# Chunk 1's DMA transposes made to wait for chunk 2's softmax-weight spread: a study of one ordering change

## The chip, the cores and the metric

The kernel runs on one core of one Trainium2 chip. The metric is the device time of one execution in microseconds (us). Each median below is over all runs of one kernel in one comparison. A ratio is the mean time of one kernel's fast runs over that of the other's fast runs of the same rounds on the same chip, so it is not quite the ratio of the two medians quoted beside it. Runs of three or more rounds are given with a 95% interval of that ratio.

## The reference, cut to what matters

Two layers with a residual each, over 2048 positions of width 1024 in bf16:

```python
def _A_ref(x, wqkv, wo):            # 32 heads of 32; each position attends to 8 earlier ones, 2 apart
    ...
    logits = jnp.where(mask[None, None, :, :], logits, -1000000000.0)
    attn = _softmax(logits, axis=-1)
    o = jnp.einsum('bhsw,bhswd->bhsd', attn, vg)
    return (...)(o, 0, 2, 1, 3).reshape(B, S, D) @ wo

def _B_ref(x, w_in, w_sp, b_sp, w_out):
    z = _gelu(jnp.einsum('bsd,df->bsf', x, w_in))
    z1 = z[..., :Fh].copy()
    z2 = _layernorm(z[..., Fh:], axis=-1)
    g = jnp.einsum('ts,bsf->btf', w_sp, z2) + b_sp[None, :, None]
    return jnp.einsum('bsf,fd->bsd', z1 * g, w_out)

h  = x + _A_ref(_layernorm(x, axis=-1), A_wqkv, A_wo)
h2 = h + _B_ref(_layernorm(h, axis=-1), B_w_in, B_w_sp, B_b_sp, B_w_out)
```

The layer norm of `h` is called LN2 here.

## The kernel before: the parts that the change and the argument touch

The positions are worked in four chunks of 512 (four blocks of 128 each). The author plans the order of the instructions of the tensor engine (PE), the vector engine (DVE) and the scalar engine (ACT) with a small list scheduler, `Order`: each `add` names an engine, an estimated duration, a function that emits the instructions, and the operations it depends on. `dma_op` is an operation on a pretend engine "DMA". The functions are called in the order of their planned starts. The queues of SP and GpSimd (POOL), which issue most transfers, the build orders itself. `behind(i, j, why)` makes instruction i wait on the chip until transfer j has landed.

The three places that matter are the spread of the softmax weights, the transposes of LN2's output, and the stores of z1:

```python
# attention(c): softmax weights of a chunk, copied from 32 rows per quarter to 128 rows, in two halves
for q in (0, 2, 1, 3):
    i_ = (A.dma_start if hw == 0 and q < 2 else dma_w)(
        st["AB"][:, hw, q]..., st["attn"][32 * q:32 * q + 32, ws, :]....to_broadcast([H, 4, 512]))
    if hw == 0:
        st["sent", q] = i_
    else:
        behind(i_, st["sent", 1], "second half behind the first")
        behind(i_, st["sent", 3], "second half behind the first")
...
# head(c): LN2's normalised output is transposed by DMA, one block at a time, from SP
for il in range(TPC):
    def tr(il=il):
        ...
        G["hntr"] = nc.sync.dma_start_transpose(hnTs[c][:, il], st["hnc"][:, il, :]....)
        if c == NCH - 3:
            behind(G["hntr"], G["ld", c + 2, 1], "transposing and loading by turns")
    trs.append(dma_op(4.0, tr, [nd[il]]))
...
# b_z1(c): ACT evicts an accumulator through GELU into one of four buffers, SP stores it
def ev(fp=fp):
    z1s = l1.tile([P, 2, CH], BF16, name="z1s", tag="xn", bufs=4)
    A.activation(z1s[:], G["accy", c, fp][:], ACTF.Gelu_apprx_tanh)
    last_store[:] = [dma(z1_d[2 * fp:2 * fp + 2, ...], z1s[:])]
```

The transposed LN2 output of chunk 1 (`hnT`) is read by PE in `b_z2(1)`, block by block. PE's accumulators (`acc`) are three buffers, each freed by an eviction on ACT or DVE.

## Time and profile before

| What | Value | Where it is read |
|---|---|---|
| time | 723.0 us median (722.67 to 724.84, 6 runs) | the runs beside the changed kernel's |
| PE busy | 716.1 us of a 721.3 us span, clock 1.0 | the page |
| unbroken row of matmuls in the chain | 7.42 to 718.32 us | the chain, in order of time |
| waits of PE | 1.3 and 0.7 us, both in the start-up | who waited for whom |
| four transposes of chunk 1 | issued from 240.57 to 247.56 us | timeline |
| PE's first use of block 0, of block 1 | 254.15, 260.21 us | timeline |

First, two lines of the page of the kernel before: PE's busy time, and the engines' shares of the chain of work that ended last.

```profile
PE 716.1 (99%) x3449; PEld 364.0 (50%) x3449; DVE 412.2 (57%) x442; ACT 236.1 (33%) x301; POOL 63.8 (9%) x78
...
PE 99%; DVE 0%; DMA 0%; ACT 0%; issue 0%
```

The same chain in order of time (start, duration, what; L666 is the output projection, L736 is z2, L786 is z1, L896 is the spatial mix), around the place of the change and later:

```profile
234.35 19.96 PE acc L786 x92
254.32 24.21 PE acc L736 x128
...
286.30 13.81 PE acc L666 x64
...
428.19 48.35 PE acc L896 x224
```

The pieces join without a hole: 234.35 + 19.96 is 254.31, and so on. 224 matmuls in 48.35 us are 215.9 ns each. The Trainium skill ("TensorE: Matmul & The Clock Gate", "Step-by-step: what each phase is for") has about 216 ns for the gap of back-to-back matmuls of 512 columns, and this trace agrees. PE neither waits nor runs slowly, so as long as its work stays the same, no other engine's saving can shorten this row.

Now the place itself: the timeline of the kernel before from 200 to 262 us (start, duration, engine, line, operation, output and input, count; in brackets, how long the engine was idle before and what ended that; SPq and ACTq are the instruction queues of SP and ACT, here issuing transfers).

```profile
240.57 6.99 SPq L708 DMA_TRANSPOSE hnT<-hb  x4
240.78 1.26 ACTq L558 DMA_DIRECT2D AB<-attn  x2
...
241.16 1.12 POOL L558 DMA_DIRECT2D AB<-attn  x2 [8.81 <-PE acc L786]
...
246.90 2.17 POOL L558 DMA_DIRECT2D AB<-attn  x4 [4.62 <-DVE l3var L628]
...
247.66 5.96 SPq L793 DMA_DIRECT2D z_d<-z1s  x5
...
249.91 2.28 DVE L604 TENSOR_TENSOR oT<-vT,AB 128x4096 bf16<-128x4096 bf16 x1
...
252.21 1.02 ACT L792 ACTIVATE z1s<-acc 128x1024 bf16<-128x1024 f32 x1 [3.67 <-DMA z_d<-z1s]
...
254.15 3.62 PE L736 MATMUL acc<-win_1453,hnT 128*128 128x512 bf16 x16
...
260.21 2.10 PE L736 MATMUL acc<-win_1453,hnT 128*128 128x512 bf16 x9
```

The four transposes stand in a row on SP from 240.57 us; the trace's list of SP's waits has them released by the load of chunk 3's keys (`kT`). The first half of the spread goes out beside them (ACT's queue from 240.78, POOL's from 241.16), and its second half follows at 246.90, once the first has landed. The bracket on that line names DVE, but by the code these transfers depend on the first half and not on that DVE instruction (in e5 below the same bracket names the transfer). Five stores of z1 stand behind the transposes, and ACT waits 3.67 us for the landing of one of them before the eviction at 252.21. DVE starts on the spread weights at 249.91 without a wait. The four transposes took 4.0 to 5.5 us from issue to landing; those of the other chunks took 2.9 us in the median.

### The profile page before, as it was taken

Reading aid. Unit: us, or ns where it says so; the run is one execution under the profiler, and the core shown is the slowest. Engines: PE = TensorE matmul, PEld = TensorE weight load, DVE = VectorE, ACT = ScalarE, POOL = GpSimd, SP = SyncE. Lnnn points to the kernel's source line nnn. Section 1 sums busy time; section 2 is a strip of 40 time slices with the busy share of each in tenths; the row PEclk is TensorE's granted clock in tenths of the full one; section 3 lists DMA queues with packets and bytes.
Section 4 is the critical chain, followed back from the end, with each engine's and each line's share of the span. In section 5 each row is a group of like instructions: output and inputs, shape, how many; then the busy total and the mean of one; then the engine's idle time right before and its main releaser. Section 6 shows DMA issues by size and latency. Waiting matters only on the chain.

```text
span 721.3 us, 8471 instructions
## 1 busy us (share of the span) xinstructions
PE 716.1 (99%) x3449; PEld 364.0 (50%) x3449; DVE 412.2 (57%) x442; ACT 236.1 (33%) x301; POOL 63.8 (9%) x78
## 2 busy tenths in 40 slices
PE   8999999999999999999999999999999999999998
PEld 4666665666644454445445444444444444444444
DVE  5898799979998999887961203222222222222222
ACT  4389452532447595766725420000000000000000
POOL 0011400012002302201113000000000000000000
PEclk9999999999999999999999999999999999999999
DMA  9995765567662942642336989463015311120002
GB/s 330 268 286 141 219 153 163 162 199 247 239 238 86 238 174 90 234 117 59 143 119 195 279 227 306 144 149 114 30 44 135 126 32 45 33 88 11 1 16 72
DMA packets 119990, 107.35 MB, mean 149 GB/s; under 512 B 72896, under 2 KB 98272, under 8 KB 119952
## 3 DMA queue, kind: packets, MB, share of 16 engines
q1 hardware_dynamic: 110624, 73.95, 34.9%
q0 software_dynamic: 7888, 31.43, 13.1%
q10 hardware_dynamic: 1440, 1.44, 0.8%
q8 instruction: 27, 0.44, 0.3%
q14 instruction: 11, 0.09, 0.0%
HBM read 55.09 MB, written 30.74 MB: 119 GB/s over the span
## 4 chain that ended last, share of the span: by engine, by line
PE 99%; DVE 0%; DMA 0%; ACT 0%; issue 0%
PE acc L896 27%; PE acc L393 21%; PE acc L736 13%; PE acc L786 13%; PE acc L918 13%; PE acc L666 8%; PE acc L303 2%; PE L L501 1%; DMA xp<-in_A_x_dram 0%; PE tpa L265 0%; DVE xn L253 0%; DVE bnst L241 0%; DVE bnst L242 0%; DVE ot L920 0%; ACT xnT L267 0%
## 5 line engine op out<-in xcount | busy, mean ns | idle before, releaser
L736 PEld LDWEIGHTS <-hnT 128*128 128x128 bf16 x512 | 50.0, 98 | 47.3 <-issue 0.4
L918 PEld LDWEIGHTS <-zg 128*128 128x128 bf16 x462 | 45.2, 98 | 51.8
L449 DVE TENSOR_TENSOR prod<-qT,kT 128x4096 bf16<-128x4096 bf16 (+1 forms) x32 | 68.2, 2152 | 2.7 <-ACT kT L399 1.5
L604 DVE TENSOR_TENSOR prod<-vT,AB 128x4096 bf16<-128x4096 bf16 (+1 forms) x32 | 64.3, 2022 | 0.8
L606 DVE TENSOR_TENSOR oT<-oT,prod 128x4096 bf16<-128x4096 bf16 (+1 forms) x32 | 64.5, 2018 | 0.1
L920 DVE TENSOR_TENSOR ot<-acc,hr 128x1024 bf16<-128x1024 f32 (+2 forms) x18 | 19.9, 1106 | 73.1 <-PE acc L918 73.1
L918 PE MATMUL acc<-wout_a,zg 128*128 128x512 bf16 (+1 forms) x264 | 58.2, 373 | 0.0
L736 PE MATMUL acc<-win_1453,hnT 128*128 128x512 bf16 x256 | 58.2, 379 | 0.0
L393 PE MATMUL acc<-xnT,wk 128*128 128x512 bf16 x256 | 56.3, 379 | 0.0
L786 PE MATMUL acc<-hnT,win_1657 128*128 128x512 bf16 x256 | 56.2, 379 | 0.0
L666 PE MATMUL acc<-wo_sb,oT 128*128 128x512 bf16 x256 | 56.1, 379 | 0.0
L393 PE MATMUL acc<-xnT,wv 128*128 128x512 bf16 x256 | 55.9, 379 | 0.0
L404 ACT CAST stg<-acc 128x1024 bf16<-128x1024 f32 x36 | 36.4, 1011 | 58.4 <-PE acc L393 51.5
L393 PEld LDWEIGHTS <-wk 128*128 128x128 bf16 x256 | 36.9, 145 | 18.6 <-issue 0.4
L393 PEld LDWEIGHTS <-wv 128*128 128x128 bf16 x256 | 37.0, 145 | 18.2
L918 PE MATMUL acc<-wout_b,zg 128*128 128x512 bf16 (+1 forms) x198 | 44.4, 373 | 0.0
L736 PE MATMUL acc<-win_1550,hnT 128*128 128x512 bf16 (+1 forms) x256 | 44.2, 326 | 0.0
L786 PE MATMUL acc<-hnT,win_1663 128*128 128x512 bf16 x192 | 42.4, 379 | 0.0
L393 PE MATMUL acc<-xnT,wq 128*128 128x512 bf16 x192 | 42.2, 379 | 0.0
L792 ACT ACTIVATE z1s<-acc 128x1024 bf16<-128x1024 f32 x28 | 28.5, 1020 | 38.6 <-PE acc L786 30.2
L666 PEld LDWEIGHTS <-oT 128*128 128x128 bf16 x256 | 25.0, 98 | 30.2
L786 PEld LDWEIGHTS <-win_1657 128*128 128x128 bf16 x256 | 25.0, 98 | 30.0 <-issue 0.4
(267 smaller groups left out, 968.3 us busy)
## 6 DMA issues: line engine op xcount, KB each, us to landing
z_d<-z1s SPq DMA_DIRECT2D x28, 256.0 KB, 2.5
z1c<-z_d SPq DMA_DIRECT2D x28, 256.0 KB, 2.8
z_d<-u SPq DMA_DIRECT2D x12, 448.0 KB, 2.5
xr<-in_A_x_dram SPq DMA_DIRECT2D x16, 256.0 KB, 2.7
h_d<-hb SPq DMA_DIRECT2D x16, 256.0 KB, 2.0
hr<-h_d SPq DMA_DIRECT2D x16, 256.0 KB, 2.8
out_dram<-ot SPq DMA_DIRECT2D x15, 256.0 KB, 2.0
kT<-qkv_d_58 POOLq DMA_DIRECT2D x3, 1056.0 KB, 9.1
```

Source lines behind the costliest of these rows:

```text
L393: G["mmins", c, xi, dp] = T.matmul(G[key][:, j, :], wv[:, kt, dl, :], xnT[c][:, kt, :], start=(kt == 0), stop=(kt == KT - 1))
L404: A.copy(stg[:], G[key][:])
L449: V.tensor_tensor(qs[w]["prod"][:, d0:d1], qT[:, d0:d1], kT[:, d0:d1, o:o + CH], op=ALU.mult)
L604: V.tensor_tensor(dst[:, :, sq].rearrange("p d (q s) -> p d q s", q=nq), vv, abb, op=ALU.mult)
L606: V.tensor_tensor(oTs[c][:, :, sq], oTs[c][:, :, sq], pvs[w, q0][:, :, sq], op=ALU.add)
L666: T.matmul(st["acc", il][:, nh, :], oTs[c][:, dl, il * P:(il + 1) * P], wo_sb[:, dl, nh * CH:(nh + 1) * CH], start=(dl == 0), stop=(dl == ...
L736: T.matmul(accf[:, n0:n1], hnTs[c][:, il, kt, :], wins[hf][:, kt, n0:n1], start=(kt == 0), stop=(kt == KT - 1))
L786: T.matmul(G["accy", c, fp][:, j, :].rearrange("p (a b) -> p a b", a=TPC), wt[:, kt, f0 * P:(f0 + 1) * P], hnTs[c][:, :, kt, :], start=(kt ...
L792: A.activation(z1s[:], G["accy", c, fp][:], ACTF.Gelu_apprx_tanh)
L896: m_ = T.matmul(acc[:, j, :], z2sb[a][:, f * P:(f + 1) * P], wspT[:, a, :], start=(a == 0), stop=(a == NT - 1))
L918: T.matmul(acc[:, m0 - n0:m1 - n0], zg[:, f, il * P:(il + 1) * P], wt[:, f0, m0:m1], start=(f == 0), stop=(f == NF - 1))
L920: V.tensor_tensor(ot[:, n0:n1], acc[:, 0:n1 - n0], hr[:, n0:n1], op=ALU.add)
```

## The change

Its intent is to keep transposes and the spread out of each other's way: all of chunk 1's transposes but the first are held until the first half of chunk 2's spread has landed. There are two edits: the planner is told of the new order, and the transposes get a wait on the chip.

```diff
-                            st["sent", q] = i_
+                            st["sent", q] = G["sent", c, q] = i_
...
                     abs_[0, 0] = abs_[0, 1] = dma_op(3.6, lambda: None, [sent])
+                    if c == NCH - 2:
+                        for t_ in G["hnTs", c - 1][1:]:
+                            t_.deps.append((abs_[0, 0], 0.0))
...
                 if c == NCH - 3:
                     behind(G["hntr"], G["ld", c + 2, 1], "transposing and loading by turns")
+                    for q in (1, 3) if il else ():
+                        behind(G["hntr"], G["sent", c + 1, q], "transposing and spreading by turns")
```

## The prediction

> What bounds the kernel. The tensor engine. The page gives PE 716.1 us busy of a 721.3 us span (99%) at granted clock 1.0. The chain that ended last is PE for 99% of the span: one unbroken row of matmuls from 7.42 to 718.32 us. The list of waits has two of PE, 1.3 and 0.7 us, both in the start-up. In the chain 224 matmuls of 512 columns take 48.35 us in the spatial mix (215.9 ns each) and 64 take 13.81 us in the output projection (215.8 ns). The Trainium skill ("TensorE: Matmul & The Clock Gate", "Step-by-step: what each phase is for") gives about 216 ns for this back-to-back gap; the trace agrees. So a change that removes no matmul can hardly gain. It can lose, by starving PE.
>
> What the change does. It adds and removes no work. It moves three DMA transposes (chunk 1's LN2 output, blocks 1 to 3) behind the landing of the first half of chunk 2's spread.
> - Before (timeline of the SP queue): the four transposes start at 240.57 us, released by the load of chunk 3's kT, and are issued over 6.99 us, up to 2.32 us each, landing in 4.0 to 5.5 us; those of other chunks take about 1.29 us each to issue and land in 2.9 us. The four spread transfers go out from 240.8 us on, in the same stretch; the second half is issued at 246.90. The table of stretches has the DMA engines full from 242 to 248 us (share 1.1 to 1.2). The Trainium skill ("DMA: Bandwidth & Descriptors", "Issuing engines are not separate DMA queues") says that DMAs of all issuers interleave on the same 16 engines; these numbers agree.
> - After, as estimated from these: the first half lands around 245.5, the second is issued about 1 us earlier than now. The three transposes are issued from 245.5 to 249.5 and have landed by 252.5, 3 us later than now.
>
> What hangs on it.
> - PE first reads block 0 at 254.15 us (it doesn't wait for the spread) and block 1 at 260.2: some 7 us of slack.
> - DVE first uses the spread weights at 249.91 us, after other work with no wait. An earlier landing gains nothing.
> - Five stores of z1 stand behind the transposes on SP (from 247.66). If they stay behind, they go about 2 us later. ACT already waits 3.67 us for one before the eviction at 252.21. That eviction and the next (256.67) may go 1 to 2 us later; PE needs the accumulators that they free at 257.6 and 260.2. About 2.5 us are to spare. If stores pass ahead of the waiting transposes, ACT's wait shrinks instead.
> - The order on PE, ACT and DVE should not change: their consumers come well after the transposes' new end.
>
> So nearly nothing of it is on the critical path. Predicted 723.0 us; 8 in 10 between 722.2 and 724.2. Chances: faster by over 2% 0.003, within 2% 0.987, slower by over 2% 0.01.
>
> What would show it. Right: PE 99% of the chain, no new PE wait; transposes 1 to 3 issued after about 245.5 at about 1.3 us each; the second half issued before 246.9. Wrong: a PE gap around 257 to 262 us, released by an eviction.
>
> What would make it wrong. The build orders the SP and GpSimd queues itself: a reordering far from here (a later load put behind the waiting transposes) could starve PE by a few us. So could ACT falling behind by over 2.5 us.

## The result, and the profile after

The changed kernel takes 722.81 us median (722.67 to 723.09, 6 runs), against 723.0 us (722.67 to 724.84, 6 runs) for the kernel before on the same rounds. The ratio is 0.9993, with a 95% interval from 0.998 to 1.0006. The two are the same.

A comparison of the instruction order of the two builds shows how small the change is: PE, DVE, ACT and POOL issue the same instructions in the same order. On SP six neighbouring transfers of 230 are reordered: `tr tr tr store store store` after the first transpose became `store store tr tr store tr`.

The page of the changed kernel, the same two lines:

```profile
PE 716.6 (99%) x3449; PEld 364.2 (51%) x3449; DVE 412.1 (57%) x442; ACT 236.3 (33%) x301; POOL 64.1 (9%) x78
...
PE 99%; DVE 0%; DMA 0%; ACT 0%; issue 0%
```

The chain in order of time (the lines have moved: L669 is the projection, L741 z2, L791 z1, L901 the spatial mix):

```profile
233.99 19.96 PE acc L791 x92
253.95 24.21 PE acc L741 x128
...
427.82 48.35 PE acc L901 x224
```

Piece by piece the durations are those of before (but for one projection ahead of the change, at 203.54 us, which took 13.90 instead of 13.81 us). Everything here starts about 0.37 us earlier, and that was won far ahead of the change: the chain has the query, key and value matmuls (L393) begin at 22.55 instead of 23.01 us, the first input transfer having taken 2.68 instead of 2.79 us. The waits of PE are down to one of 1.3 us in the start-up.

The timeline of the changed kernel from 239 to 262 us:

```profile
240.07 1.24 SPq L711 DMA_TRANSPOSE hnT<-hb  x1
...
240.46 1.25 ACTq L558 DMA_DIRECT2D AB<-attn  x2
...
240.79 1.12 POOL L558 DMA_DIRECT2D AB<-attn  x2 [8.59 <-PE acc L791]
241.40 2.06 SPq L798 DMA_DIRECT2D z_d<-z1s  x2
...
245.76 3.17 SPq L711 DMA_TRANSPOSE hnT<-hb  x2
...
246.29 2.17 POOL L558 DMA_DIRECT2D AB<-attn  x4 [4.38 <-DVE l3var L631]
...
249.54 2.28 DVE L607 TENSOR_TENSOR oT<-vT,AB 128x4096 bf16<-128x4096 bf16 x1
249.97 1.61 SPq L711 DMA_TRANSPOSE hnT<-hb  x1
...
250.58 1.02 ACT L797 ACTIVATE z1s<-acc 128x1024 bf16<-128x1024 f32 x1 [2.43 <-PE acc L791]
...
253.78 3.62 PE L741 MATMUL acc<-win_1453,hnT 128*128 128x512 bf16 x16
...
259.84 2.54 PE L741 MATMUL acc<-win_1453,hnT 128*128 128x512 bf16 x11
```

Locally the change did what it says. The first transpose goes out as before, the next two wait until 245.76 us, the last goes at 249.97. Two z1 stores have passed ahead (241.40). ACT no longer waits for a store: the eviction that stood at 252.21 us after a wait of 3.67 us now stands at 250.58 and waited for PE only. Yet the spread itself gained next to nothing. From the first POOL transfer to the second half it took 5.74 us (241.16 to 246.90) and now takes 5.50 us (240.79 to 246.29). PE starts on block 0 at 253.78 and on block 1 at 259.84 us, as early in its row as before.

### The profile page after: what moved, and what is told of

Same layout as the page of the kernel before. It is cut to its first block, busy times and chain, and to the rows that moved or that the text cites. A ratio compares the mean times of both kernels' runs of the same rounds, so it can differ in the third digit from the quotient of the medians.

```text
span 720.9 us, 8469 instructions
## 1 busy us (share of the span) xinstructions
PE 716.6 (99%) x3449; PEld 364.2 (51%) x3449; DVE 412.1 (57%) x442; ACT 236.3 (33%) x301; POOL 64.1 (9%) x78
## 4 chain that ended last, share of the span: by engine, by line
PE 99%; DVE 0%; DMA 0%; ACT 0%; issue 0%
PE acc L901 27%; PE acc L393 21%; PE acc L741 13%; PE acc L791 13%; PE acc L923 13%; PE acc L669 8%; PE acc L303 2%; PE L L501 1%; DMA xp<-in_A_x_dram 0%; PE tpa L265 0%; DVE bnst L241 0%; DVE xn L253 0%; DVE bnst L242 0%; DVE ot L925 0%; PE tp_152 L265 0%; ACT sd_145 L247 0%
## 5 line engine op out<-in xcount | busy, mean ns | idle before, releaser
L741 PEld LDWEIGHTS <-hnT 128*128 128x128 bf16 x512 | 50.0, 98 | 47.3 <-issue 0.4
L741 PE MATMUL acc<-win_1453,hnT 128*128 128x512 bf16 x256 | 58.2, 379 | 0.0
L393 PE MATMUL acc<-xnT,wk 128*128 128x512 bf16 x256 | 56.3, 379 | 0.0
L791 PE MATMUL acc<-hnT,win_1657 128*128 128x512 bf16 x256 | 56.2, 379 | 0.0
L669 PE MATMUL acc<-wo_sb,oT 128*128 128x512 bf16 x256 | 56.1, 379 | 0.0
L393 PE MATMUL acc<-xnT,wv 128*128 128x512 bf16 x256 | 55.9, 379 | 0.0
L393 PEld LDWEIGHTS <-wk 128*128 128x128 bf16 x256 | 36.9, 145 | 18.6 <-issue 0.4
L393 PEld LDWEIGHTS <-wv 128*128 128x128 bf16 x256 | 37.0, 145 | 18.2
L741 PE MATMUL acc<-win_1550,hnT 128*128 128x512 bf16 (+1 forms) x256 | 44.2, 326 | 0.0
L791 PE MATMUL acc<-hnT,win_1663 128*128 128x512 bf16 x192 | 42.4, 379 | 0.0
L393 PE MATMUL acc<-xnT,wq 128*128 128x512 bf16 x192 | 42.2, 379 | 0.0
L669 PEld LDWEIGHTS <-oT 128*128 128x128 bf16 x256 | 25.0, 98 | 30.3 <-DVE oT L609 0.4
L791 PEld LDWEIGHTS <-win_1657 128*128 128x128 bf16 x256 | 24.9, 98 | 30.0 <-issue 0.4
```

The source lines that it names most:

```text
L393: G["mmins", c, xi, dp] = T.matmul(G[key][:, j, :], wv[:, kt, dl, :], xnT[c][:, kt, :], start=(kt == 0), stop=(kt == KT - 1))
L669: T.matmul(st["acc", il][:, nh, :], oTs[c][:, dl, il * P:(il + 1) * P], wo_sb[:, dl, nh * CH:(nh + 1) * CH], start=(dl == 0), stop=(dl == ...
L741: T.matmul(accf[:, n0:n1], hnTs[c][:, il, kt, :], wins[hf][:, kt, n0:n1], start=(kt == 0), stop=(kt == KT - 1))
L791: T.matmul(G["accy", c, fp][:, j, :].rearrange("p (a b) -> p a b", a=TPC), wt[:, kt, f0 * P:(f0 + 1) * P], hnTs[c][:, :, kt, :], start=(kt ...
```

## The experiments

Twelve runs of ten kernels were made, on three chips, each beside the kernel before (e10 and e11 are e6 and e7 again). Unless said otherwise a diff is against the changed kernel. The results first:

| Kernel | Median us (runs) | Before, same rounds | Ratio, 95% interval |
|---|---|---|---|
| e1_plan_only | 722.96 (4) | 722.95 (7) | 1.0001, 0.9986 to 1.0017 |
| e2_all_four | 722.98 (4) | 722.95 (7) | 0.9998, 0.9983 to 1.0013 |
| e3_second_1to3 | 722.93 (4) | 722.95 (7) | 0.9996, 0.9981 to 1.0011 |
| e4_second_all | 723.08 (4) | 722.95 (7) | 0.9999, 0.9982 to 1.0016 |
| e5_spread_alone | 724.25 (4) | 723.16 (7) | 0.9994, 0.9946 to 1.0043 |
| e6_less_pe_before | 721.95 (4) | 723.16 (7) | 0.9967, 0.992 to 1.0014 |
| e7_less_pe_after | 722.43 (4) | 723.16 (7) | 0.9966, 0.9908 to 1.0023 |
| e8_no_turns | 727.4 (4) | 723.16 (7) | 1.0045, 0.999 to 1.01 |
| e9_over_edge | 730.67 (4) | 723.05 (11) | 1.0103, 1.009 to 1.0116 |
| e10_less_pe_before | 721.82 (6) | 723.05 (11) | 0.9989, 0.9976 to 1.0002 |
| e11_less_pe_after | 723.39 (6) | 723.05 (11) | 0.9996, 0.9984 to 1.0008 |
| e12_less_pe_late | 716.85 (4) | 723.05 (11) | 0.9914, 0.9901 to 0.9926 |

The theory to be tested has two parts. PE's row is unbroken, so nothing can be gained; and the moved transposes have slack, so nothing is lost. The rivals are that a local gain and a local loss cancel, that a late transpose costs time even before PE wants it, and that the full PE row hides a gain which another kernel could have.

### e1: the planner's half alone

```diff
-                    for q in (1, 3) if il else ():
-                        behind(G["hntr"], G["sent", c + 1, q], "transposing and spreading by turns")
```

> Half of the change: the planner is told that transposes 1 to 3 come after the spread, but no transfer waits for it. Comparing the instruction order of the two builds, all five engines issue exactly what the kernel before issues. Theory (only the waits act): 722.9 us, and the local picture of before: four transposes in a row from about 240.5 us, ACT waiting about 3.7 us for a z1 store before the eviction near 252 us. Rival (the planner's dependence alone moves something): the stores pass ahead of the transposes and that ACT wait is gone. It also shows how much two runs of the same instruction stream differ.

Measured: 722.96 us. The four transposes stand in a row again (240.02 to 247.57 us), and ACT waits 4.3 us for a z1 store. The planner's half has no effect at all, since the build orders SP's queue itself; it reordered the stores only when it saw the waits. What e1 gives is a measure of repetition: with the same instruction stream as the kernel before, POOL's first transfer and the second half are 6.09 us apart (240.93 to 247.02) where the profile of before has 5.74. The changed kernel's 5.50 is not clear of that, and e12 below, whose instructions at this place are those of the changed kernel, has 6.36 (240.88 to 247.24).

### e2 and e3: more waiting

e2 lets the first transpose wait too:

```diff
-                        for t_ in G["hnTs", c - 1][1:]:
+                        for t_ in G["hnTs", c - 1]:
...
-                    for q in (1, 3) if il else ():
+                    for q in (1, 3):
```

> The change carried to all four transposes: block 0 waits for the first half of the spread too. PE reads block 0 at 253.8 us. Theory (slack): block 0 lands around 250 us, 4 us early, PE shows no wait, 722.9 us within 0.3. Rival (transposes and spread do each other real harm, and the free first transpose keeps the gain small): the spread's second half goes out a further 0.5 us or more earlier and the time falls by more than 0.3 us.

e3 lets transposes 1 to 3 wait for the second half of the spread instead of the first (`sent2` are its four transfers; the planner's entry `issued`, which takes the place of the change's own entry, only sees to it that the transposes are emitted after them):

```diff
+                            G["sent2", c, q] = i_
...
-                    for q in (1, 3) if il else ():
-                        behind(G["hntr"], G["sent", c + 1, q], ...)
+                    for q in range(4) if il else ():
+                        behind(G["hntr"], G["sent2", c + 1, q], ...)
```

> Twice the wait: transposes 1 to 3 wait until the second half of the spread has landed (about 252 us) instead of the first (about 245.7). PE reads block 1 at about 259.9 us. Theory (slack of some 7 us): block 1 lands around 256, PE shows no wait, 722.9 us within 0.3. Rival (a late transpose costs time even when PE is not yet there, through the queue of SP and the stores behind it): 724 us or more, with ACT waiting on z1 stores.

Measured: 722.98 and 722.93 us. In e2 the transposes start at 245.83 us; in e3 the last three start at 252.07. In both PE has only its start-up waits. Neither rival holds: a later transpose costs nothing as long as PE is not there yet, and freeing the spread of the first transpose as well does not make it clearly quicker (POOL's 240.92 to 246.31 is 5.39 us; the changed kernel has 5.50).

### e4 and e9: looking for the edge

e4 is e3 without the exception for block 0 (the planner's list, not shown, loses it too):

```diff
-                    for q in range(4) if il else ():
+                    for q in range(4):
```

> Over the edge on purpose: all four transposes wait until the second half of the spread has landed. Theory (a wait costs only what it overshoots the moment PE needs the block): the second half lands at about 252 us, block 0 about 3 to 4 us later, near 255.5, where PE wants it at 253.8: a PE gap of 1.5 to 3 us released by a transpose, and the time rises by that, to 724.3 to 726, for PE never catches up. Rival (there is slack elsewhere that swallows it): a gap in PE but the time still within 0.5 us of 722.9.

Measured: 723.08 us, and no gap. The expectation was wrong on a landing time. The transposes start at 251.24 us, and with no spread or store beside it (the DMA share from 251 to 252 us is 0.00) the first takes 2.7 us to land instead of the assumed 3 to 4. Block 0 is there at 251.24 + 2.7 = 253.94 us, and PE starts on it at 254.03:

```profile
251.24 6.51 SPq L713 DMA_TRANSPOSE hnT<-hb  x4
...
254.03 4.16 PE L743 MATMUL acc<-win,hnT 128*128 128x512 bf16 x18
```

So e4 stands right on the edge. e9 goes over it: all four transposes wait until the first store of z2, which is issued about 254 us, has landed.

```diff
+                    behind(G["hntr"], G["z2store"], "transposing behind the first store of z2")
...
-                    dma(z2_d[i * P:(i + 1) * P, :], z2[:])
+                    zs_ = dma(z2_d[i * P:(i + 1) * P, :], z2[:])
+                    if i == 0:
+                        G["z2store"] = zs_
```

The change's own waits are taken out, and the planned duration of these transposes is cut to 0.6 us so that the planned order of PE, ACT and DVE stays the same (a comparison of the builds confirms it).

> Over the edge for certain, as waiting for the whole spread just failed to be (block 0 then landed about 254.0 us, right where PE wanted it): all four transposes wait until the first store of z2 (issued about 253.8 us) has landed, near 256.5. Theory (a wait is free up to the moment PE needs the block, and costs its overshoot in full after that): block 0 lands about 259.5 us, PE has one gap of 5 to 6 us there, released by a transpose, and the time is 728 to 729. Rival (other slack swallows part of a PE gap): the same gap and a time of 726 or less.

Measured: 730.67 us, 7.62 us more than the kernel before beside it, and more than the 728 to 729 that the theory gave. No slack swallowed anything; on the contrary, the loss is larger than the gap. The longest wait of PE in e9, from the list of who waited for whom (total, times, longest):

```profile
PE acc L737 <- DMA hnT<-hb: 5.5, 1, 5.5
```

And the busy time of the engines in stretches around it (stretch; its length; busy time of PE, PE's weight loads, DVE, ACT and POOL with the instructions counted; PE's granted clock; DMA share; GB/s):

```profile
256.00:258.00 2.00, 0.00 (x0) 0.00 (x0) 2.00 (x2) 2.00 (x2) 0.00 (x0) 0.74 0.66 239
258.00:260.00 2.00, 0.35 (x1) 0.13 (x2) 1.97 (x2) 0.50 (x1) 0.00 (x0) 0.50 1.04 235
260.00:262.00 2.00, 2.00 (x6) 0.76 (x5) 2.00 (x2) 0.00 (x0) 0.00 (x0) 0.50 1.45 167
262.00:264.00 2.00, 2.00 (x6) 0.70 (x5) 1.97 (x2) 0.00 (x0) 0.00 (x0) 0.55 0.87 108
264.00:266.00 2.00, 2.00 (x12) 0.98 (x10) 2.00 (x2) 0.61 (x1) 0.00 (x0) 1.00 1.03 362
```

The gap is 5.5 us. During it the granted clock falls to 0.50, and it stays there until PE has worked again for about 4 us: between 260 and 262 us PE shows 6 matmuls, between 264 and 266 us, at full clock, 12. A clock of 0.55 over 262 to 264 us is 0.50 up to 263.8 and 1.0 after that. PE is back at work at 259.65 us by the timeline; half speed from there to 263.8 us loses about 2.1 us of work. Then 5.46 of gap and 2.1 of slow clock make 7.5 us, and 7.62 were measured. The Trainium skill ("TensorE: Matmul & The Clock Gate", "HAM oscillation — how this bites in real kernels") warns of idle gaps of PE longer than about 3.4 us for this reason. The trace agrees with the mechanism, a gap of 5.5 us followed by a clock of 0.50; when the clock falls is taken up in the last section. So the theory had the gap right and lacked the clock.

### e5: the spread with nothing beside it

All four transposes wait for the first half, as in e2, and so do the three z1 stores that would go out in the same stretch.

```diff
+            def store(fp=fp):
+                last_store[:] = [dma(z1_d[2 * fp:2 * fp + 2, ...], G["z1s", c, fp][:])]
+                if c == 0 and fp in (1, 2, 3):
+                    for q in (1, 3):
+                        behind(last_store[0], G["sent", NCH - 2, q], "storing and spreading by turns")
```

> The spread's first half with nothing beside it: all four transposes, and the three z1 stores that would go out in the same stretch, wait until it has landed. In the kernel before, the second half is issued 6.12 us after the first transfer of the first half went out, in the changed kernel 5.83 us. Theory of the prediction (contention held the spread up): with all of it gone the second half follows after about 4.5 to 5 us. Rival (most of that time is the issue and landing of four transfers by themselves; for chunk 3, with no transpose beside it, it is 5.6 us): 5.4 to 5.7 us. Both expect 722.9 us.

Measured: the second half follows 4.57 us after ACT's first transfer (240.65 to 245.22), where the kernel before took 6.12 and the changed kernel 5.83 us. Counted from POOL's first transfer it is 4.23 us, against 5.39 (e2) to 6.40 (e3) in the kernels above. The four transfers of the first half land 2.7 to 3.1 us after issue, against 3.8 to 4.6 in the kernel before.

```profile
240.65 1.21 ACTq L558 DMA_DIRECT2D AB<-attn  x2
...
240.99 1.12 POOL L558 DMA_DIRECT2D AB<-attn  x2 [9.07 <-PE acc L792]
...
244.74 6.26 SPq L712 DMA_TRANSPOSE hnT<-hb  x4
245.22 2.17 POOL L558 DMA_DIRECT2D AB<-attn  x4 [3.11 <-DMA AB<-attn]
...
249.78 2.28 DVE L608 TENSOR_TENSOR oT<-vT,AB 128x4096 bf16<-128x4096 bf16 x1
```

So contention does hold up the spread, as the prediction had it, and the rival falls. But the change did not take the contention away. It exchanged it: in the place of the transposes two stores of z1 went out at 241.40 us, 256 KB each by the page's list of issues. The time of e5 shows no gain either. Its profiled run took 722.87 us with PE free of waits, and DVE starts on the spread weights at 249.78 us although they landed earlier than before. ACT waits 5.5 us there for a held z1 store before its eviction at 253.87 us, and that costs nothing either. The executions on this chip scattered (722.87 to 725.63; the kernel before 722.86 to 730.12), so the median says little.

### e6, e7, e10, e11: is a gain or a loss hidden under PE's row?

If PE's row alone hides the effect, it should appear when PE has less to do. In two output tiles of chunk 0's first half (just before 254 us) only one of eight slices is summed; the result is wrong. 28 matmuls at 0.2159 us, that is 6.04 us, fall away. The edit is applied to the kernel before (e6, e10) and to the changed one (e7, e11).

```diff
+                    few = c == 0 and fp in (5, 6)
                     for kt in range(4 * kh, 4 * kh + 4):
+                        if few and kt:
+                            continue
```

> Kernel before with 28 of 3449 matmuls left out just ahead of this place (two output tiles of chunk 0's first half sum one of eight slices; the result is wrong on purpose). At 0.216 us each that is 6.0 us of PE. Theory (PE alone bounds, all else has slack of 6 us): 717 us. Rival (the DVE chain of attention follows close behind: its last addition of chunk 2 ends at 284.6 us, and PE starts the output projection on it at 286.1 us): PE catches up with DVE and the time falls by 1.5 to 3 us only, with a PE gap at the projection released by DVE.

> The same 28 matmuls left out of the changed kernel. If the change has a gain or a loss that the full PE row only hides (sooner spread, ACT no longer waiting for a store), it shows here as a difference of over 0.5 us from the kernel before with the same cut. Theory (the change moves nothing that bounds): the same time within 0.3 us. Rival (hidden gain): faster than it by 0.5 us or more; (hidden loss, transposes 1 to 3 late for a PE that comes 6 us sooner): slower.

> The kernel before with 28 matmuls (6.0 us of PE) left out ahead of this place once more, since the first pair ran on a chip whose executions spread by several us. Theory (as the first run's trace has it: DVE's chain and the chain spread, GpSimd, ACT, PE stand 1 to 2 us behind the PE row): 721.3 to 722.2, not 717.

> The changed kernel with the same cut, on the same chip as the kernel before with it. Theory (the change does not move a chain that stands close behind): within 0.4 us of it. Rival (hidden gain or loss): apart by 0.5 us or more, with different PE gaps.

Measured, kernel before with the cut: 721.95 and 721.82 us. Of 6.04 us only 1.2 arrive in both (723.16 - 721.95 and 723.05 - 721.82). The theory that PE alone bounds falls for this place, and the rival holds: others stand close behind PE's row here. The waits of PE in e10:

```profile
PE acc L736 <- ACT z1s L795: 2.4, 2, 2.1
PE acc L666 <- DVE oT L606: 1.7, 1, 1.7
```

PE catches up with two others: with DVE's attention chain at the output projection, and with ACT's evictions. Changed kernel with the cut: 722.43 and 723.39 us. Its profiles have a longer gap of PE, and a chain that runs through the spread. The longest wait of PE in e11:

```profile
PE acc L741 <- ACT z1s L800: 4.6, 2, 4.3
```

And from the chain of e11 in order of time:

```profile
241.72 6.27 DMA AB<-attn
...
248.58 2.17 POOL AB L558 x4
250.75 2.63 POOL l3rstd L633
...
253.47 1.29 POOL l3nb L638
...
256.57 1.86 ACT u L770
258.44 0.92 ACT z1s L800
...
259.39 20.61 PE acc L741 x96
```

POOL issues the spread's second half, for which the first has to land, and after that computes the reciprocal deviation of LN3 (the layer norm inside `_B_ref`; `l3rstd`) and its bias (`l3nb`); ACT normalises with them, and behind that stands the eviction that frees PE's accumulator. This is a real path from the landing of the spread to PE. (e7's chain is the same from POOL's second half on; before that it names an instruction of DVE instead of the landing.) In the kernel as it is, the path ends in time.

What the two pairs do not settle is whether the change makes that path longer. The medians are 0.48 us apart in the first pair, where the theory allowed 0.3 and the rivals asked for 0.5, and 1.57 us in the second, where the theory allowed 0.4. But the ratios to the kernel before hardly differ (0.9967 and 0.9966 in the first pair, 0.9989 and 0.9996 in the second), and the executions of both kernels fall into two heaps: the kernel before with the cut took over 723 us in 3 of 10 executions, the changed one with the cut in 6 of 10. All nine of these show a mean clock of 0.995 to 0.998; of the other eleven, three do (0.998) and eight show 1.0. So the upper heap goes with a spell of slow clock, as after the gap of e9, and it occurs in both kernels.

The profiles do not settle it either, for they compare the heaps and not only the kernels: both of the changed kernel are of the upper heap (723.42 and 724.6 us), both of the kernel before are of the lower one (722.1 and 721.47). In them PE's longest gap was 2.1 us in e6 and e10 and 4.3 us in e7 and e11; in e11 the clock was at 0.50 from 258 to 264 us, as in e9. The longer gap has two parts: the second half left 6.74 and 7.11 us after POOL's first transfer (e7, e11) instead of 6.23 and 6.34 (e6, e10), and `l3rstd` took 3.04 and 2.67 us on POOL instead of 1.35 and 1.24. Where PE is not cut at this place, `l3rstd` varied from 1.18 to 2.16 us without following the change (1.25 before, 1.49 after, 1.22 in e12, 2.16 in e5). A hidden gain is not to be seen; a hidden loss is left open.

### e12: the same cut where nobody stands close behind

```diff
-                for a in range(NT):
+                n_a = 2 if c == NCH - 1 and fp == 5 else NT
+                for a in range(n_a):
```

Again 28 matmuls fall away, now in the last spatial mix. (The sum is wrong, but the result still passed the comparison with the reference.)

> As many matmuls (28, 6.0 us of PE) left out of the changed kernel, but in the last spatial mix, where PE's row is served by loads alone (wrong result on purpose). Theory (it depends on the place how far others stand behind PE; here far): the whole 6.0 us, 716.8 us within 0.4. Rival (the two cuts before gained little because a matmul left out is worth less than 0.216 us anywhere): 720 or more.

Measured: 716.85 us, 6.20 us less than the kernel before, with only start-up waits of PE. In the chain the piece of the last spatial mix is shorter (the kernel before has x224 in 48.35 us there):

```profile
645.45 42.30 PE acc L902 x196
```

Here a matmul left out is worth its full time. So the unbroken row of PE means two different things: in the last stage everything else is far ahead; around 254 to 286 us a cut of 6.04 us brings 1.2, because DVE's chain and ACT's evictions come due right after.

### e8: without the older turn

The kernel before already holds chunk 1's transposes behind the load of chunk 3's keys. e8 takes that away (the diff is against the kernel before):

```diff
-                if c == NCH - 3:
-                    behind(G["hntr"], G["ld", c + 2, 1], "transposing and loading by turns")
...
-            if c == NCH - 1:
-                for t_ in G["hnTs", c - 2]:
-                    t_.deps.append((d_k, 0.0))
```

> Kernel before without its older wait of the same sort: chunk 1's transposes no longer wait for the load of chunk 3's keys, so they go out when their data is ready, from about 231 us, beside that load. Theory (slack, only now in the other direction): block 0 is there some 10 us sooner, no gain, 722.9 us within 0.3; the load of the keys takes longer. Rival (the turns matter): the load comes late for DVE, which needs keys at about 241 us, the DVE chain slips by 1 us or more and PE waits at the projection: 724 us or more.

Measured: 727.4 us, and no run of it under 725.94; the rounds scattered too much for the interval to leave 1 out. The profile shows the loss (span 724.2 us against 721.3 in the profile of the kernel before). It is of an execution at clock 1.0; the two slowest of the four, 728.79 and 730.9 us, show a mean clock of 0.995. Its timeline:

```profile
228.63 16.43 SPq L705 DMA_TRANSPOSE hnT<-hb  x4
...
245.56 4.50 DVE L446 TENSOR_TENSOR prod<-qT,kT 128x4096 bf16<-128x4096 bf16 x2 [4.52 <-DMA kT<-qkv_d]
```

The waits of PE in e8:

```profile
PE acc L663 <- DVE oT L603: 1.7, 1, 1.7
...
PE acc L731 <- ACT z1s L787: 1.1, 1, 1.1
```

The transposes now start at 228.63 us and take 13.7 us to land in the median; the keys' load beside them takes 14.4 us instead of 9.1. DVE waits 4.5 us for the keys, its chain slips, and PE waits 1.7 us for it at the projection and 1.1 us for an eviction. A comparison of the builds finds no other change of order than the transposes' place on SP. So by the profiled runs taking turns with this load is worth about 3 us. Taking turns with the spread is worth nothing, because there nobody on PE's row was yet waiting for the transfer that was held up.

## Why the prediction was right

- "A change that removes no matmul can hardly gain": right, 722.81 against 723.0 us, with the chain of PE the same piece by piece. e12 adds that a matmul less is worth its time where PE alone bounds. e6 and e10 limit the statement: around the place of the change PE is the bound by 1.2 us only, with DVE's chain and ACT's evictions behind it. The prediction looked at PE's row alone and didn't see this. Nor did it look at the path from the spread through POOL and ACT to PE; that this path ended in time was luck.
- "Some 7 us of slack" for blocks 1 to 3: right in its use. In the profile block 1 was issued at 245.76 and took 4.3 us, so it was there at 250.1 us, 9.8 us before PE used it at 259.84. e3 holds it until 252.07 for nothing, e4 finds the edge for block 0, and e9 shows what lies beyond.
- "If stores pass ahead of the waiting transposes, ACT's wait shrinks instead": this branch came true. The wait of 3.67 us is gone, without effect on the time, since the accumulator was not wanted yet.
- "The second half is issued about 1 us earlier": wrong in size, and with no effect on the time. It was 5.50 instead of 5.74 us after POOL's first transfer, within what one stream varies (5.74 to 6.34 in four profiles with SP's order of before at this place, 5.50 to 7.11 in four with the changed one; the two slowest of these are those of e7 and e11). The step that failed is the estimate that the first half would then have the DMA engines nearly to itself; z1's stores took the freed place. e5 takes those away too and gets 4.23 us.
- "Issued at about 1.3 us each and landed by 252.5": half right. The issues took 1.24, 1.88 and 1.62 us, and the last block landed at 249.97 + 4.3 = 254.3 us. The transposes meet the second half of the spread and the stores instead of the first half.

## What to carry to other kernels

Before two kinds of transfer are made to take turns, ask who waits for the one that is to be protected: the load of the keys had DVE waiting behind it and its turn is worth about 3 us by the profiles; nobody on PE's row was yet waiting for the spread, and its turn is worth nothing. Holding one transfer back frees the engines for whatever else is in the queue, so look at what will move up. And a PE row without a gap can have other engines about 1 us behind it; cut some PE work in a trial, at the place in question, before counting on a gain there. When two kernels' profiles are compared, look first whether they come from the same heap of executions.

## What the Trainium skill lacked or had wrong

- "TensorE: Matmul & The Clock Gate", "What's actually happening": the clock is said to fall after an idle window of about 3.4 us. Here it fell earlier and later than 3.4 us into a gap. In e9 PE's row ends at 254.20 us and the stretch from 256 to 258 us has a mean clock of 0.74, so the fall came at about 256.96, 2.8 us into the gap. The same working gives 2.2 us in e11 (the row ends at 255.07 us, mean clock 0.81 from 256 to 258) and 4.2 us in e7 (254.69 us, 0.71 from 258 to 260). A gap of 2.1 us (e10) left the clock at 1.0. The page does say that the windows are free-running, and the spells at 0.50 lasted 6.8 us in e9 and e11 and 3.4 us in e7.
- The same page tells what the slow clock costs a kernel that idles in every tile, but has no measured example of one gap in a long row: here 2.1 us on top of a gap of 5.46 us (e9).
- "DMA: Bandwidth & Descriptors", "Rules for kernel authors", says that a transpose next to ordinary DMAs needs nothing. No wait was needed for a right result in e8 either, but the page has no figure for what the other transfers cost it in time: a transpose landed in 2.7 us alone (the first of e4), in 4.0 to 5.5 us beside the spread (the kernel before), and in 13.7 us in the median beside the loads of queries and keys, where the keys' own landing went from 9.1 to 14.4 us (e8).
